# Three loads under way at a time, and two rows spread by GpSimd, in a fused RWKV-6 and mixture-of-depths kernel

## The chip, the cores and the metric

The kernel runs on one core of one Trainium2 chip. The metric is the device time of one execution in microseconds (us), taken as the median of several executions; lower is better. The engines have short names in the profile: PE is TensorE (PEld its weight loads), DVE VectorE, ACT ScalarE, POOL GpSimd and SP SyncE, which here only issues DMAs.

## What is computed

The reference has two parts, one behind the other. The first is a recurrence over 768 tokens for 4 batches and 8 heads of width 48:

```python
for t in range(S):
    cur = np.einsum('bhd,bhe->bhde', u[None] * kt, vt)
    y[:, :, t] = np.einsum('bhd,bhde->bhe', rt, state + cur)
    state = wt[:, :, :, None] * state + np.einsum('bhd,bhe->bhde', kt, vt)
```

Its result, laid out as 4 x 768 rows of 384, goes into the second part, in which the 128 tokens with the highest scores of each batch pass through a small network:

```python
scores = np.einsum('bsd,d->bs', x, w_gate)
top_idx = np.argpartition(-scores[b], capacity)[:capacity]
h = np.maximum(x[b, top_idx] @ w1, 0.0)
g = 1.0 / (1.0 + np.exp(-scores[b, top_idx]))
out[b, top_idx] = x[b, top_idx] + g[:, None] * (h @ w2)
```

Two small inputs matter for the change: `u`, 384 numbers that multiply r times k for every token, and `w_gate`, 384 numbers for the score. Both are needed as the same row in all 128 partitions.

## The kernel before

Time is cut into 24 chunks of 128 tokens (4 batches of 6), and the recurrence is done chunk by chunk with matmuls. One long loop at the end of the function, `for n in range(-4, N)`, is a software pipeline: iteration n works on chunk n's result and, ahead of it, on the stages of chunks n+1 to n+4. The order of the instructions on every engine is the order of the calls, written out by hand under `manual_schedule`.

The stages of one chunk, in order, with the lines by which the profile knows them:

- `load` (L110) issues one DMA of 192 KB from SP for each of w, k, r and v. `loads(n)` asks for v of chunk n+1, k and r of n+3 and w of n+4; iteration n calls `loads(n + 3)` near its end (a little differently in the first few). There are 96 such loads. Five w buffers and six each for k with r, and for v, rotate; a load waits until its buffer's last reader is done.
- `lnw` (L148) takes the logarithm of w on ACT. `sums` (L171) adds it up over the tokens on PE, and ACT takes the exponential (L173). `totals` (L183, L187) makes one line of 384 numbers on ACT and spreads it by a small DMA, issued from ACT, into `all_buf`. `without` (L194, DVE) and `falls` (L200, ACT) make the second exponential.
- `scaled` (L232, DVE) multiplies k and r by the exponentials. `own_products` (L209, L210) computes r times k times `u_bc` on POOL; `own_sum` (L217) adds it up per head on DVE; `own_values` (L224) multiplies by v on POOL.
- `turned` (L243, L245) transposes on PE and copies on ACT. `scores` (L259), `fresh` (L275), `masked` (L287, DVE), `states` (L300, L305 on DVE, L307 on POOL), `from_state` (L318) and `from_chunk` (L335) are the chunk's matmuls and what lies between them.
- `result` (L349, L355) adds the parts on DVE, forms the scores with `wg_bc`, and issues the chunk's store from ACT (L359).

From n = 6 on, steps of the second part (choosing rows, gathering them by a POOL DMA, two matmul layers at L485 and L495) are mixed in between by `mix`; those of the last batch make a tail with no chunk work beside it. From n = 7 on, eight DMAs of 384 KB from SP (L610) bring the weights of the network.

All DMA issues of SP and of ACT share eight semaphores, given out in turn when the program is compiled. An issue on either engine therefore also waits until the earlier transfer with the same semaphore, as a rule the eighth in front in the order of the program, has landed.

Before the loop ACT issues the loads of the rows `u_row` and `wg_row` into partition 0. POOL fills constants with memset and iota (L539 to L561). The rows are spread to all partitions inside the loop's first two iterations by `to_all` (L155, L156): PE multiplies a column of ones by the row into PSUM, and ACT copies the result to `u_bc` and `wg_bc`.

Of the kernel before, what the change touches and what calls it, by code (L numbers as in the profile page):

```python
# [9 lines left out]
FP32 = mybir.dt.float32  # L10
# [7 lines left out]
L = 128  # L18
# [4 lines left out]
def _rows(ap, n):  # L23

    return dataclasses.replace(ap, ap=[[0, n]] + [list(x) for x in ap.ap])
# [10 lines left out]
def kernel(  # L36
# [14 lines left out]
    nc = tc.nc  # L51
# [3 lines left out]
    C = H * D  # L55
# [13 lines left out]
    consts = ctx.enter_context(tc.tile_pool(name="consts", bufs=1))  # L69
# [6 lines left out]
    psM = ctx.enter_context(tc.tile_pool(name="psM", bufs=1, space=PSUM))  # L76
# [9 lines left out]
    u_bc = consts.tile([L, H, D], FP32)  # L86
    wg_bc = consts.tile([L, C], FP32)
    u_row = consts.tile([1, H, D], FP32)
    wg_row = consts.tile([1, C], FP32)
    ones_row = consts.tile([1, L], FP32)  # L90
    kr_bufs = [consts.tile([L, 2, H, HB], FP32, name=f"kr_buf{i}") for i in range(4)]
    line_bufs = [consts.tile([1, 2, HB, HP], FP32, name=f"line_buf{i}") for i in range(3)]
    p_bufs = [psP.tile([L, 2, 512], FP32, name=f"ps_p{i}") for i in range(2)]
    all_bufs = [consts.tile([L, HP], FP32, name=f"all_buf{i}") for i in range(6)]

    work = {n: {} for n in range(N)}
    latest = {}

    def load(name, n):
        if not 0 <= n < N:  # L100
            return
        b, ci = chunks[n]
        x, bufs = dict(w=(w, 5), k=(k, 6), r=(r, 6), v=(v, 6))[name]
        if name == "k":
            work[n]["kr"] = lev.tile([L, 2, H, D], FP32, tag="kr", name="kr", bufs=bufs)
        if name in "kr":
            t = work[n]["kr"][:, "kr".index(name)]
        else:
            t = lev.tile([L, H, D], FP32, tag=name, name=name, bufs=bufs)
        nc.sync.dma_start(  # L110
            out=t, in_=x[b, :, ci * L:(ci + 1) * L, :].rearrange("h t d -> t h d")
        )
        work[n][name] = t

    def loads(n):
        load("v", n + 1)
        load("k", n + 3)
        load("r", n + 3)
        load("w", n + 4)
# [18 lines left out]
    row = setup.tile([L, L], INT32)  # L138
# [5 lines left out]
    def lnw(n):  # L144
        if 0 <= n < N:
# [2 lines left out]
            nc.scalar.activation(  # L148
                out=t["lw"], in_=t.pop("w").rearrange("p h d -> p (h d)"), func=AF.Ln
            )  # L150

    def to_all(out, row):

        ps = psM.tile([L, 512], FP32, tag="f", name="ps_b")
        nc.tensor.matmul(ps[:, 0:C], ones_row, row, start=True, stop=True)  # L155
        nc.scalar.copy(out=out, in_=ps[:, 0:C])  # L156

    def sync(ins, on, why):

        tc.add_manual_dep(  # L160
            ins.ins, on.ins.name,
            mybir.DependencyInfo(mybir.DependencyClass.Sync, mybir.DependencyReason.DATA),
            reason=why,
        )

    def sums(n):
        if not 0 <= n < N:
# [81 lines left out]
    def half(i, n=HB):  # L249
        return slice(HB * i, HB * i + n)  # L250
# [201 lines left out]
    def gates(b):  # L452

        xe, gate = chosen[b][2], chosen[b][4]
        own = mod.tile([L, 1], FP32, name="own", bufs=2)
        scr = lev.tile([L, C], FP32, tag="scr", name="scr")
        nc.vector.tensor_tensor_reduce(
            out=scr, in0=xe, in1=wg_bc, scale=1.0, scalar=0.0, op0=ALU.mult, op1=ALU.add,
            accum_out=own,
        )  # L460
        neg = mod.tile([L, 1], FP32, name="neg", bufs=2)
        nc.vector.scalar_tensor_tensor(
            out=neg, in0=own, scalar=-1.0, in1=own, op0=ALU.mult, op1=ALU.min
        )
        yield
        nc.scalar.activation(out=neg, in_=neg, func=AF.Exp)
        yield
        den = mod.tile([L, 1], FP32, name="den", bufs=2)
        nc.vector.tensor_scalar_add(out=den, in0=neg, scalar1=1.0)
        nc.vector.reciprocal(out=den, in_=den)  # L470
        nc.vector.scalar_tensor_tensor(
            out=gate, in0=own, scalar=0.0, in1=neg, op0=ALU.is_ge, op1=ALU.max
        )
        nc.vector.tensor_mul(gate, gate, den)
        yield
# [55 lines left out]
    with tc.manual_schedule():  # L531
        nc.scalar.dma_start(out=u_row, in_=_rows(u, 1))
        nc.scalar.dma_start(out=wg_row, in_=_rows(moe_w_gate, 1))
        nc.scalar.preload_act_table_set("natural_log_exp_and_others")
        loads(-4)
        loads(-3)
        loads(-2)

        nc.gpsimd.memset(ones_row, 1.0)  # L539
        nc.gpsimd.iota(row, pattern=[[1, L]], base=0, channel_multiplier=0)  # L540
        nc.gpsimd.iota(col, pattern=[[0, L]], base=0, channel_multiplier=1)
        nc.vector.tensor_tensor(out=tri, in0=col, in1=row, op=ALU.is_ge)
        nc.vector.tensor_tensor(out=ident, in0=col, in1=row, op=ALU.is_equal)
        for t in kr_bufs:
            nc.vector.memset(t[:, :, :, D:HB], 0.0)
        for t in line_bufs:
            nc.gpsimd.memset(t[:, :, D:HB, :], 1.0)
        nc.vector.tensor_tensor(out=behind[:, 0:L], in0=col, in1=row, op=ALU.is_lt)
        for i in (0, 1):
            nc.vector.tensor_copy(out=mask[half(i)], in_=behind[half(i), half(i)])  # L550
            nc.vector.memset(p_bufs[i], 0.0)
        nc.vector.tensor_copy(out=slots, in_=row)
        nc.vector.memset(ones, 1.0)
        nc.vector.memset(ones_f, 1.0)
        nc.gpsimd.memset(behind[:, L:S], 1.0)
        nc.gpsimd.iota(count, pattern=[[-L, NCH]], base=S - 1, channel_multiplier=-1)
        nc.vector.tensor_copy(out=behind_n, in_=count)
        nc.gpsimd.iota(
            number[:, :, :, 0], pattern=[[S, B], [L, NCH]], base=0, channel_multiplier=0
        )  # L560
        nc.gpsimd.iota(  # L561
            number[:, :, :, 1], pattern=[[0, B], [0, NCH]], base=0, channel_multiplier=1
        )
        nc.vector.tensor_copy(out=ids, in_=number)

        for n in range(-4, N):
            what = ("", "", "")
            if n >= NCH:
                b, j = n // NCH - 1, n % NCH
                what = plan[j]  # L570
                if j == 0:
                    steps["s"] = select(b)
                if j == rank_at:
                    steps["x"] = chosen_rows(b, "m" if b == B - 2 else "f")
                if j == gate_at and b > 0:
                    steps["g"] = gates(b - 1)
            if n == N - 1:
                what = ("g", "", "g")
            from_state(n)
            own_values(n + 1)  # L580
            totals(n + 3)
            without(n + 3)
            lnw(n + 4)
            if n == -4:
                to_all(u_bc.rearrange("p h d -> p (h d)"), u_row.rearrange("o h d -> o (h d)"))
            scores(n + 1)
            fresh(n + 1)
            from_chunk(n)
            turned(n + 2, "K")
            turned(n + 2, "R")  # L590
            falls(n + 3)
            if n == -3:
                to_all(wg_bc, wg_row)
            masked(n + 1)
            states(n + 1)
            result(n)
            mix(what[0])
            if n >= 2 * NCH and n % NCH == 0:
                steps["f"] = forward(n // NCH - 2)
            sums(n + 4)  # L600
            mix(what[1])
            scaled(n + 3)
            mix(what[2])
            own_products(n + 3)
            own_sum(n + 2)
            for m in range(max(n - 1, -4) if n <= AHEAD else n, n if n < AHEAD else n + 1):
                loads(m + AHEAD)
            if 0 <= n - WEIGHTS_AT < len(weights):
                to, of = weights[n - WEIGHTS_AT]
                nc.sync.dma_start(out=to, in_=of)  # L610

        steps["s"] = select(B - 1)
        steps["x"] = run(steps["x"], chosen_rows(B - 1, "r"))
        mix("ffsxffsssssf")
        steps["f"] = forward(B - 2, "rmf")
        total = setup.tile([L, 1], FP32)
        nc.vector.tensor_reduce(out=total, in_=guard, axis=AX.XY, op=ALU.add)
        mix("ffffxxxff")
        ps = bank("f")
        nc.tensor.matmul(ps[0:1, 0:1], total, ones_f, start=True, stop=True)  # L620
        wide = setup.tile([1, 1], INT32)
        mix("xx")
        nc.vector.tensor_scalar(
            out=wide, in0=ps[0:1, 0:1], scalar1=LIMIT, scalar2=0.5, op0=ALU.is_le, op1=ALU.is_lt
        )
        steps["g"] = gates(B - 2)
        mix("gggff")
        wide = nc.values_load(wide, min_val=0, max_val=1)
        mix("fffffxffff")
        steps["g"] = gates(B - 1)  # L630
        mix("ggg")
        for _ in forward(B - 1, "mrf"):
            pass
# [104 lines left out]
```

## Time and profile before

| | |
|---|---|
| median of 3 runs | 187.31 us (186.99 to 192.36) |
| time of the profiled execution | 188.42 us |
| its span, first to last instruction | 186.5 us |
| PE busy | 162.9 us (87%) |
| DVE busy | 137.4 us (74%) |
| POOL busy | 92.9 us (50%) |
| ACT busy | 84.7 us (45%) |
| loads and weights (queue q1): share of the 16 DMA engines over the span | 57.5% |
| stores and small lines (queue q10): the same | 8.1% |
| landing of a load after its issue, median by tensor | 4.3 to 5.0 us, the shortest 3.0 us |

"Busy" is the time in which an engine had an instruction running. The digit rows of the profile cut the span into 40 slices of 4.66 us and give the busy share of each slice in tenths. The chain of waits goes back from the last instruction to whatever released it, and so on to the start; "issue" in it is time for which the profile shows no cause. A line of the timeline has the start and the duration in us, the engine and line, the operation, what it writes and reads, and in brackets the idle time before it and what ended it. "SPq" and "ACTq" are the sequencers that issue DMAs; the duration there is that of issuing, not of the transfer.

### The profile page before, as it was taken

The numbers are of one execution on the slowest core, as the hardware profiler recorded it, in microseconds if no ns is written. First come the engines' busy times: TensorE is split into PE (matmuls) and PEld (weight loads), VectorE is DVE, ScalarE is ACT, GpSimd is POOL, SyncE is SP. The second block draws the span as 40 slices with busy tenths as digits, with TensorE's granted clock in tenths as the row PEclk, the third lists the DMA queues.
The fourth block names the chain that finished last, engine by engine and source line by source line (L and its number), as shares of the span: only waits on it lengthen the run. The fifth ranks groups of instructions, "written<-read, shape, count | busy, mean of one in ns | idle before, by whom it ended". The sixth has DMA issues, their size and how long they took to land.

```text
span 186.5 us, 8415 instructions
## 1 busy us (share of the span) xinstructions
PE 162.9 (87%) x3590; PEld 131.2 (70%) x3590; DVE 137.4 (74%) x326; ACT 84.7 (45%) x239; POOL 92.9 (50%) x114
## 2 busy tenths in 40 slices
PE   4989959878995989895887999999999999999990
PEld 1358838657784777674777988768899867977940
DVE  6636978786879899998698789779999964942100
ACT  4476643565673736453753547257633303111200
POOL 4036776463765466589076255854756540131102
PEclk9999987999999999999999999999999999999997
DMA  6999987998999998999999999996111112020101
GB/s 125 210 197 187 179 171 169 212 212 182 206 189 202 225 231 223 183 241 226 215 208 260 226 197 270 219 190 150 43 49 46 47 48 84 0 91 4 42 9 46
DMA packets 109425, 28.98 MB, mean 155 GB/s; under 512 B 103362, under 2 KB 108996, under 8 KB 109380
## 3 DMA queue, kind: packets, MB, share of 16 engines
q1 hardware_dynamic: 102528, 22.03, 57.5%
q10 hardware_dynamic: 6340, 4.77, 8.1%
q0 software_dynamic: 512, 1.57, 2.5%
q8 instruction: 30, 0.49, 1.1%
q14 instruction: 15, 0.12, 0.2%
HBM read 22.81 MB, written 5.51 MB: 152 GB/s over the span
## 4 chain that ended last, share of the span: by engine, by line
PE 57%; issue 17%; POOL 5%; DMA 5%; DVE 4%; ACT 4%; ACTq 1%; POOLq 1%; DVEq 0%
PE ps_p L335 10%; PE ps_t L243 9%; PE ps_f L485 8%; PE ps_x L171 6%; PE ps_f L495 6%; PE ps_p L318 6%; PE ps_p L259 5%; PE ps_p L275 4%; DMA kr<-in_r_dram 3%; DMA all_buf<-line_buf 2%; POOL rk L209 2%; DVE kr_buf L232 1%; POOL vo L224 1%; PE ps_e L373 1%; PE ps_r L406 1%
## 5 line engine op out<-in xcount | busy, mean ns | idle before, releaser
L209 POOL TENSOR_TENSOR rk<-kr 128x384 f32<-128x384 f32 x24 | 24.0, 1001 | 51.6 <-DVE kr_buf L232 23.6
L335 PE MATMUL ps_p<-v,sc 64*64 64x48 f32 x768 | 28.7, 219 | 7.9 <-issue 4.2
L232 DVE TENSOR_TENSOR kr_buf<-kr,e 128x768 f32<-128x768 f32 x24 | 25.0, 1043 | 13.6 <-ACT e L200 11.9
L335 PEld LDWEIGHTS ps_p<-v,sc 64*64 64x64 f32 x768 | 25.4, 135 | 9.3 <-issue 4.9
L243 PE MATMUL ps_t<-ident,kr_buf 128*128 128x128 f32 x192 | 28.3, 292 | 2.0 <-issue 2.0
L245 ACT COPY Kt<-ps_t 128x512 f32<-128x512 f32 x24 | 14.0, 582 | 26.9 <-PE ps_t L243 26.9
L171 PE MATMUL ps_x<-lw,tri 128*128 128x384 f32 x48 | 23.3, 570 | 3.1 <-ACT lw L148 2.2
L243 PEld LDWEIGHTS ps_t<-ident,kr_buf 128*128 128x128 f32 x192 | 22.0, 147 | 4.5 <-issue 2.4
L210 POOL TENSOR_TENSOR rk<-rk,u_bc 128x384 f32<-128x384 f32 x24 | 24.0, 1002 | 1.9
L485 PEld LDWEIGHTS ps_f<-xeT,w 128*128 128x128 f32 x192 | 22.6, 192 | 1.3
L485 PE MATMUL ps_f<-xeT,w 128*128 128x128 f32 x192 | 23.4, 277 | 0.0
L495 PE MATMUL ps_f<-w,hid 128*128 128x384 f32 x64 | 22.2, 490 | 0.0
L224 POOL TENSOR_TENSOR vo<-v,own 128x384 f32<-128x384 f32 x24 | 20.2, 843 | 1.8 <-DVE own L217 1.8
L318 PEld LDWEIGHTS ps_p<-s,Rt 48*64 48x64 f32 x704 | 14.0, 138 | 10.0 <-issue 4.5
L148 ACT ACTIVATE lw<-w 128x384 f32<-128x384 f32 x24 | 12.6, 526 | 16.1 <-issue 5.5
L318 PE MATMUL ps_p<-s,Rt 48*64 48x48 f32 x704 | 17.3, 226 | 0.9 <-issue 0.5
L355 DVE CUSTOM_DVE_ANT_0 scr<-x,wg_bc 128x384 f32<-128x384 f32 x24 | 17.3, 722 | 0.8
L506 POOL DMA_INDIRECT out_dram<-ye,idx x4 | 4.7, 1173 | 26.3 <-DVE ye L503 15.6
L259 PE MATMUL ps_p<-Rt,Kt 48*64 48x64 f32 x768 | 17.7, 229 | 0.0
L173 ACT ACTIVATE e<-ps_x 128x384 f32<-128x384 f32 x24 | 11.7, 489 | 12.8 <-DVE score L355 3.5
L387 DVE SCALAR_TENSOR_TENSOR ahead<-every,score,behind 128x768 bf16<-128x768 f32 (+5 forms) x24 | 15.3, 679 | 2.6 <-ACT every L376 2.6
L287 DVE TENSOR_TENSOR sc<-ps_p,mask 128x512 f32<-128x512 f32 x24 | 16.3, 680 | 0.5 <-PE ps_p L275 0.5
(79 smaller groups left out, 247.5 us busy)
## 6 DMA issues: line engine op xcount, KB each, us to landing
w<-in_w_dram SPq DMA_DIRECT2D x24, 192.0 KB, 4.5
kr<-in_k_dram SPq DMA_DIRECT2D x24, 192.0 KB, 4.9
kr<-in_r_dram SPq DMA_DIRECT2D x24, 192.0 KB, 5.0
v<-in_v_dram SPq DMA_DIRECT2D x24, 192.0 KB, 4.3
out_dram<-x ACTq DMA_DIRECT2D x24, 192.0 KB, 3.8
w<-in_moe_w_dram SPq DMA_DIRECT2D x8, 384.0 KB, 5.8
all_buf<-line_buf ACTq DMA_DIRECT2D x20, 2.0 KB, 3.5
xe<-out_dram,idx POOLq DMA_INDIRECT x4, 4.2
```

The costliest lines, as they stand in the source:

```text
L171: nc.tensor.matmul(ps[:, 0:C], tri, t["lw"], start=True, stop=True)
L209: sync(nc.gpsimd.tensor_mul(rk, t.pop("r"), t.pop("k")), latest["two"], "one port")
L210: nc.gpsimd.tensor_mul(rk, rk, u_bc)
L224: nc.gpsimd.tensor_mul(t["vo"], t["v"], t.pop("own").to_broadcast([L, H, D]))
L232: latest["two"] = nc.vector.tensor_mul(both[:, :, :, 0:D], t.pop("kr"), t.pop("e").rearrange("p q (h d) -> p q h d", d=D),)
L243: nc.tensor.transpose(ps[:, j, :], t[name][:, 2 * j:2 * j + 2, :], ident)
L259: nc.tensor.matmul(P[half(sub), par, j * HB:(j + 1) * HB], t["Kt"][half(par, D), j, half(sub)], t["Rt"][half(par, D), j, half(sub)], start ...
L318: nc.tensor.matmul(t["P"][half(sub), par, j * D:(j + 1) * D], t["Rt"][half(par, D), j, half(sub)], t["s1" if sub else "s0"][half(par, D), ...
L335: nc.tensor.matmul(t["P"][half(sub), par, j * D:(j + 1) * D], t["sc"][half(sub), par, j, :], t["v"][half(sub), 2 * j + par, :], start=(sub ...
L355: nc.vector.tensor_tensor_reduce(out=scr, in0=x, in1=wg_bc, scale=1.0, scalar=0.0, op0=ALU.mult, op1=ALU.add, accum_out=score[:, b, ci:ci ...
L485: nc.tensor.matmul(ps[:, q, :], w1[:, dc, (f0 + q) * L:(f0 + q + 1) * L], xeT[:, dc, :], start=(dc == 0), stop=(dc == NDC - 1),)
L495: nc.tensor.matmul(ps, hid[:, fc, :], w2[:, fc, :], start=(fc == 0), stop=(fc == NFC - 1))
```

## The change

`load` keeps a list of the loads' issue instructions. From the 17th load on, each load gets a dependency on the third load in front of it: it is issued after that one has landed. The weights' DMAs (L610) and ACT's DMAs are not in the list. `to_all` with its matmuls and ACT copies goes, and so does the row of ones. In its place POOL runs two `partition_broadcast` instructions ahead of the loop, after its last iota. `sync`, the helper that adds a dependency, moves up unchanged.

```diff
+    under_way = []
+    MOST = 3
+    UNLIMITED = 16
...
-        nc.sync.dma_start(
+        under_way.append(nc.sync.dma_start(
             out=t, in_=x[b, :, ci * L:(ci + 1) * L, :].rearrange("h t d -> t h d")
-        )
+        ))
+        if len(under_way) > UNLIMITED:
+            sync(under_way[-1], under_way[-1 - MOST], "loads under way")
...
-    def to_all(out, row):
-
-        ps = psM.tile([L, 512], FP32, tag="f", name="ps_b")
-        nc.tensor.matmul(ps[:, 0:C], ones_row, row, start=True, stop=True)
-        nc.scalar.copy(out=out, in_=ps[:, 0:C])
...
-        nc.gpsimd.memset(ones_row, 1.0)
...
         nc.vector.tensor_copy(out=ids, in_=number)
+        nc.gpsimd.partition_broadcast(
+            u_bc.rearrange("p h d -> p (h d)"), u_row.rearrange("o h d -> o (h d)"), channels=L
+        )
+        nc.gpsimd.partition_broadcast(wg_bc, wg_row, channels=L)
...
-            if n == -4:
-                to_all(u_bc.rearrange("p h d -> p (h d)"), u_row.rearrange("o h d -> o (h d)"))
...
-            if n == -3:
-                to_all(wg_bc, wg_row)
```

More of the change, by code (lines that the diff above doesn't have):

```diff
@@ L89 @@
     wg_row = consts.tile([1, C], FP32)
-    ones_row = consts.tile([1, L], FP32)
     kr_bufs = [consts.tile([L, 2, H, HB], FP32, name=f"kr_buf{i}") for i in range(4)]
@@ L96, with sync @@
     work = {n: {} for n in range(N)}
+    under_way = []
+    MOST = 3
+    UNLIMITED = 16
     latest = {}
+    def sync(ins, on, why):
+        tc.add_manual_dep(
+            ins.ins, on.ins.name,
+            mybir.DependencyInfo(mybir.DependencyClass.Sync, mybir.DependencyReason.DATA),
+            reason=why,
+        )
     def load(name, n):
@@ L150, in lnw @@
             )
-    def to_all(out, row):
-        ps = psM.tile([L, 512], FP32, tag="f", name="ps_b")
-        nc.tensor.matmul(ps[:, 0:C], ones_row, row, start=True, stop=True)
-        nc.scalar.copy(out=out, in_=ps[:, 0:C])
[L158 to L164, printed above, removed]
     def sums(n):
@@ L564 @@
         nc.vector.tensor_copy(out=ids, in_=number)
+        nc.gpsimd.partition_broadcast(
+            u_bc.rearrange("p h d -> p (h d)"), u_row.rearrange("o h d -> o (h d)"), channels=L
+        )
+        nc.gpsimd.partition_broadcast(wg_bc, wg_row, channels=L)
         for n in range(-4, N):
```

## The prediction

> **What bounds the kernel now.** I read the digit rows first, for the stages:
>
> ```profile
> PE   4989959878995989895887999999999999999990
> DVE  6636978786879899998698789779999964942100
> POOL 4036776463765466589076255854756540131102
> DMA  6999987998999998999999999996111112020101
> ```
>
> Up to slice 27 (some 126 us) the 16 DMA engines are nearly full and so is PE; behind it PE works alone through the second part. Queue q1 holds 57.5% of 186.5 us = 107.2 us for 96 loads and 8 weight transfers, so one transfer keeps the engines 1.03 us. A chunk of four loads and a store (8.1% of 186.5 over 24 = 0.63 us) needs 4.75 us. From chunk 3 to chunk 10 `kr_buf` (L232) starts at 22.06 and 61.83 us: 5.68 us a chunk. In the same window PE's own work for a chunk, summed from the chain's pieces (L243 1.02, L171 0.65, L318 0.61, L259 0.48, L275 0.36, L335 0.93), is 4.05 us. DMA has some 0.9 us a chunk to spare there, little more than PE.
>
> Next the chain of waits, cut to 22 to 32 us:
>
> ```profile
> 23.78 0.48 PE ps_t L243 x3
> 24.26 2.04 issue
> 26.30 0.71 PE ps_t L243 x5
> ```
>
> PE stands for 2.04 us in the middle of a row of transposes. Of such "issue" gaps the groups of L335, L243, L275 and L318 have 4.2 + 2.0 + 2.3 + 0.5 = 9.0 us, and the timeline shows none over 0.3 us after 125 us, when the loads are over.
>
> Then SP's timeline, for what limits loads today:
>
> ```profile
> 22.20 0.92 SPq L110 DMA_DIRECT2D w<-in_w_dram  x1
> 23.16 2.96 SPq L110 DMA_DIRECT2D v<-in_v_dram  x1
> 26.21 0.56 SPq L110 DMA_DIRECT2D kr<-in_k_dram  x1
> ```
>
> An issue that takes 0.4 us when nothing is queued takes 2.96: the queue is full and pushes back. And ACT's timeline:
>
> ```profile
> 92.11 0.47 ACT L183 ACTIVATE line_buf<-ps_x 1x384 f32<-1x384 f32 x1
> 93.97 0.48 ACTq L187 DMA_DIRECT2D all_buf<-line_buf  x1
> 94.49 0.52 ACT L148 ACTIVATE lw<-w 128x384 f32<-128x384 f32 x1 [1.91 <-DMA kr<-in_r_dram]
> ```
>
> ACT stood 1.91 us until an r load landed, which none of its data needs: its own DMA issue uses that load's semaphore. Late loads reach ACT through this too.
>
> Last, the prologue, POOL and DVE:
>
> ```profile
> 2.61 0.14 POOL L561 IOTA number<- 128x24 int32 x1
> 8.93 1.00 POOL L209 TENSOR_TENSOR rk<-kr 128x384 f32<-128x384 f32 x1 [6.18 <-DVE kr_buf L232]
> ...
> 13.71 0.55 DVE L217 TENSOR_REDUCE own<-rk 128x8 f32<-128x384 f32 x1
> 14.18 0.55 DVE L194 TENSOR_TENSOR less<-ps_x,lw 128x384 f32<-128x384 f32 x1
> ```
>
> POOL idles 6.18 us, from 2.75 to 8.93, so a new instruction there seems free. Chunk 0's product ends at 11.0 and DVE adds it up only at 13.71: 2.7 us more of slack. But DVE runs in order, and `less` of chunk 2, which ACT and PE need, stands right behind.
>
> **What the Trainium skill says.** "GPSIMD Engine Reference", section 2.1 (Instruction dispatch): GpSimd's instructions are software that can be loaded at run time, and the first call to a freshly loaded kernel pays about 6 us (5.95 measured) with no instruction of its own in the profile. No such load is in this trace (the iota at L540 starts 0.06 us after the memset before it), so nothing here agrees or disagrees. "DMA: Bandwidth & Descriptors", section Anatomy of one DMA: about 2.0 us of a DMA are fixed, most of it the receipt that the last byte is written. The trace agrees: the first w load is issued at 0.76, ACT uses it at 3.78, so 3.02 us, less 1.03 of transfer. "Runtime: NRT & Kernel Launch", section Instruction fetch mechanics: instructions come by DMA in blocks of 16 KiB, as a rule hidden. Queue q8 moved 30 packets, 0.49 MB, 16 KB each; PE's gaps beside full DMA engines suggest that hiding fails there.
>
> **The change part by part.** *Removed from PE and ACT.* Two pairs of matmuls (L155, 1.61 and 1.64 us a pair) and two copies of 0.46 us. The first pair runs 2.26 to 3.87, before the first `ps_x` at 4.35, which waits for w: nothing. The second ends at 7.57 where `ps_x` could have gone at 7.23 (its input is ready then): 0.3 us gained at most. ACT's copies lie in idle time; ones_row's memset was 0.19 us on an idle POOL. Take -0.3.
>
> *Added to POOL.* Two broadcasts of 384 columns. Nearest rows: an iota of 128 columns 0.22 us, so 0.66 for 384; a two-input product of 384 columns 1.00. Take 0.6 each, 1.2 together, between 0.5 and 2 us. Both rows' DMAs landed by 3.3 us (2.0 at most after issue), so they hardly wait. Alone they would end at about 4, well ahead of 8.93: nothing.
>
> *Added unseen.* The kernel used only memset, iota, tensor_tensor and indirect DMA on POOL. If partition_broadcast lives in another loaded set than tensor_tensor, POOL must load one before it and the old one after it. Price: 6 us each by the page; other transfers take longer beside full DMA engines (an all_buf line lands in 2.0 us at best, 3.5 in the median; a store 1.9 and 3.8), so I take 9, between 6 and 12. Then POOL's first product starts at 2.75 + 9 + 1.2 + 9 = 22 and DVE's L217 at 24.1, against 13.71: DVE and all behind it are 10.4 us late. With 6 us each it is 4.4, with 12 it is 16.4; with a single load 1.4. Behind POOL's stall wait `own`, `vo`, `s` (L307), and so PE and ACT. SP meanwhile runs on only until it meets buffers and semaphores that ACT has to pass, about eight transfers. What is won back: for seven chunks up to 62 us the period can fall from 5.68 to about 5.1 (4.05 of PE work and the issue gaps, near DMA's 4.75), 0.6 x 7 = 4 us. Later there is no room: DVE is at 95% in 60 to 75 us and PE at 96% from 95 to 125. Net +6, between +1 and +12.
>
> *The limit.* From load 17 (15.16 us) to the 55th (62.75) SP issued one load per 1.25 us. With three under way the rate is three per landing time: at the unloaded 3.02 us one per 1.02, no limit; at the median of all loads, 4.8 (the view of L110), one per 1.6, so 6.4 us a chunk against 5.68 and +13 us in 38 loads. Fewer in front make landings shorter, so I take the middle, 3.9, one per 1.3: +2 us, half of it hidden by data loaded ahead during POOL's stall: +1. What waits behind a held load on SP: the next loads, and from 64 us on the weights, uncounted, which keep the engines filled; a chunk then lasts some 6.4 us and needs 5.2 of loads. Who waits for SP: ACT's L148 and its issues L187 and L359. Where less is queued, instruction fetches may come sooner: a tenth of the 9.0 us, -0.5.
>
> *Sum.* -0.3 + 0 + 6 + 1 - 0.5 = +6.2. On the profiled execution, span 186.5 and time 188.42, that is 194.6; that execution is 1.1 above the median of 187.31, so I forecast 193.5.
>
> **Rivals.** *A, faster.* The broadcast needs no load, and a shorter queue cures the gaps in PE: 60% of 9.0 us and 0.3, so 181.6. For it: the gaps lie only where loads run. Against: the limit still leaves a load or two queued. It decides where landings fall to 3.1 us or so: then three under way feed a load per 1.03 us, the engines stay full, and fetches wait less. *B, slower by the limit.* No load of programs, but landings stay near 4.8 us because stores and weights share the engines: +5 to +13, 192 to 200. For it: the windows give the DMA engines a share of 0.94 or more in every stretch from 4 to 125 us but one (0.85 in 30 to 40); any gap between loads is lost for good. *C, nothing happens.* The full queue and the eight semaphores already hold loads to about four under way (issued 1.25 us apart, landing after 4.8: 3.8 on the mean), so three changes nearly nothing, and the broadcast is cheap: 187. *D, dear loads:* 12 us each: 199 to 200.
>
> **How the numbers follow.** Two program loads, with or without a little from the limit: 0.50. D: 0.08; B: 0.10; A: 0.18; C or a single load: 0.14. Two per cent, 3.7 us, is about what a measurement of this kernel can tell from no change: faster below 183.6, slower above 191.1. The forecast's own case reaches below 191.1 only with short loads, which I count under C. So faster 0.18, within 0.14, slower 0.68. The likeliest case alone spans 190 to 198. The range must take in C and the mildest of A at its lower end and all but the top of B and D at its upper: 184 to 199. Outside remain most of A (0.13) and some of B and D (0.06).
>
> **What would show it.** Right: on POOL an idle stretch of 15 us or more around the two broadcasts, the first product at 16 us or later, L217 late by as much, a `less` waiting behind it; then a period of about 5 us. Wrong: broadcasts done by 5 us and the first product at 8.9. For the limit: median landings of 3.5 to 4 us, issues no longer 2 to 3 us long, DMA digits down to 8 in 15 to 60 us; wrong if the digits stay 9 and landings stay 4.8. For A: PE's issue gaps below 4 us in sum.

## The result: slower, 199.96 us against 187.22

The changed kernel takes 199.96 us (median of 4 runs, 199.75 to 200.14); the kernel before, 187.22 us. The ratio is 1.068, 95% interval 1.066 to 1.071: 12.7 us more. The forecast was 193.5 with a range up to 199, so the direction was right, and the time lies just outside the range. Some executions of one kernel last a few per cent longer than its others: medians here and below hold all, ratios and their intervals leave those out, and a dash in the table below stands for a profile of one of them.

In the profiled execution (200.14 us, span 198.4) the lines have moved: `load` is L120, `lnw` L160, the first exponential L171, the `all_buf` line L181 and L185, `own_products` L207 and L208, `own_sum` L215, `scaled` L230, `from_chunk` L333, the store L357. First the digit rows, 40 slices of 4.96 us:

```profile
PE   1670898797697768796699996999999999999990
DVE  6530889697566999987579995757999993861201
POOL 3204957484651766549415775175477622040202
...
DMA  6999998789998799898997997962120112111101
```

Two things differ. In the fourth slice (15 to 20 us) PE and DVE stand still while the DMA engines go on. And from the eighth slice to the end of the loads DMA has 7s, 8s and 6s where it had 9s, and PE has 6s and 7s up to 100 us. The timeline of POOL and DVE around the first of these:

```profile
2.68 0.14 POOL L558 IOTA number<- 128x24 int32 x1
8.51 1.07 POOL L563 PARTITION_BROADCAST u_bc<-u_row  x1 [5.68 <-issue]
9.46 0.67 POOL L566 PARTITION_BROADCAST wg_bc<-wg_row  x1
17.37 0.98 POOL L207 TENSOR_TENSOR rk<-kr 128x384 f32<-128x384 f32 x1 [7.24 <-issue]
...
19.45 0.55 DVE L215 TENSOR_REDUCE own<-rk 128x8 f32<-128x384 f32 x1 [5.56 <-POOL rk L208]
```

POOL idles 5.68 us before the first broadcast and 7.24 us behind the second, with nothing in the timeline to wait for. The list of the instructions of L563 and of L207 has a pair of MODIFY_POOL_CONFIG, of POOL's sequencer, at the head of each of the two stretches (2.8 and 10.0 us). I read the stretches as two loads of programs. DVE's L215 starts at 19.45 where it started at 13.71, 5.7 us late, and behind it in DVE's order stands `less`, for which ACT and PE wait. For the second, the chain of waits (start, duration, what) in a stretch of the weights' loads:

```profile
74.67 6.02 DMA kr<-in_k_dram
...
80.84 4.82 DMA v<-in_v_dram
...
87.35 7.22 DMA kr<-in_k_dram
...
94.65 0.41 ACTq L357
95.06 0.05 issue
95.11 0.58 ACT e L171 x2
...
95.79 1.39 PE ps_p L333 x32
```

Loads follow one another on the path, each issued when an earlier one lands. Then comes a store's issue on ACT (L357), 0.08 us after the k load of 87.35 has landed. ACT needs nothing of that load: `kr_buf` reads it at 112.85, 18 us later. The store uses its semaphore: by the trace's semaphore numbers the DMAs of SP and ACT share eight, those of GpSimd have eight others, and at least 12 of ACT's 44 issues inside the loop start within 0.15 us of the landing of an SP load on the same semaphore. Behind the store in ACT's order stand the exponential (L171) and `seen`, a small copy out of `ps_p` between `from_state` and `from_chunk`, for which PE waits. The list of waits shows how often that happens (total us, times, longest):

```profile
PE ps_p L333 <- ACT seen L324: 9.7, 7, 2.4
ACT e L171 <- DMA kr<-in_k_dram: 6.4, 3, 3.3
ACT lw L160 <- DMA kr<-in_k_dram: 3.8, 2, 3.0
ACT lw L160 <- DMA w<-in_moe_w_dram: 2.0, 1, 2.0
ACT lw L160 <- DMA kr<-in_r_dram: 1.9, 3, 0.8
ACT lw L160 <- DMA v<-in_v_dram: 1.6, 1, 1.6
```

None of these ACT instructions reads k, r, v or a weight. With two more rows of `e` (v 0.9, r 0.8 us) ACT stood 17.4 us for transfers it doesn't use; in the kernel before it was 5.6 (v 2.1, r 1.9, w 1.0 ahead of an instruction that doesn't read it, k 0.6). PE's wait for `seen` grew to these 9.7 us from 3.7 in the kernel before:

```profile
PE ps_p L335 <- ACT seen L326: 3.7, 6, 1.9
```

### The profile page after: what moved, and what is told of

It is laid out like the page before. It is cut to its first block, busy times and chain, and to the rows that moved or that the text cites. A ratio compares the mean times of both kernels' runs of the same rounds, so it can differ in the third digit from the quotient of the medians.

```text
span 198.4 us, 8426 instructions
## 1 busy us (share of the span) xinstructions
PE 164.0 (83%) x3586; PEld 133.5 (67%) x3586; DVE 137.4 (69%) x326; ACT 84.6 (43%) x237; POOL 94.5 (48%) x115
## 4 chain that ended last, share of the span: by engine, by line
PE 35%; DMA 14%; issue 9%; DVE 4%; ACT 3%; POOL 1%; SPq 1%; POOLq 1%; ACTq 1%
DMA kr<-in_k_dram 7%; PE ps_p L333 6%; PE ps_f L483 6%; PE ps_f L493 5%; PE ps_t L241 5%; DMA kr<-in_r_dram 3%; PE ps_p L316 3%; PE ps_x L169 3%; DMA v<-in_v_dram 2%; PE ps_p L257 2%; DVE ahead L385 2%; DMA w<-in_w_dram 1%; PE ps_p L273 1%; DVE kr_buf L230 1%; DMA all_buf<-line_buf 1%
## 5 line engine op out<-in xcount | busy, mean ns | idle before, releaser
L207 POOL TENSOR_TENSOR rk<-kr 128x384 f32<-128x384 f32 x24 | 24.0, 998 | 48.4 <-DVE ahead L385 22.7
L333 PE MATMUL ps_p<-v,sc 64*64 64x48 f32 x768 | 29.3, 222 | 12.9 <-ACT seen L324 9.7
L169 PE MATMUL ps_x<-lw,tri 128*128 128x384 f32 x48 | 25.0, 608 | 14.9 <-ACT lw L160 8.5
L333 PEld LDWEIGHTS ps_p<-v,sc 64*64 64x64 f32 x768 | 26.1, 137 | 14.4 <-ACT seen L324 10.7
L230 DVE TENSOR_TENSOR kr_buf<-kr,e 128x768 f32<-128x768 f32 x24 | 25.3, 1056 | 12.8 <-ACT e L198 10.6
L241 PE MATMUL ps_t<-ident,kr_buf 128*128 128x128 f32 x192 | 30.6, 310 | 0.5 <-DVE kr_buf L230 0.5
L241 PEld LDWEIGHTS ps_t<-ident,kr_buf 128*128 128x128 f32 x192 | 24.1, 158 | 2.9 <-DVE kr_buf L230 1.0
L208 POOL TENSOR_TENSOR rk<-rk,u_bc 128x384 f32<-128x384 f32 x24 | 24.0, 1000 | 1.9
L171 ACT ACTIVATE e<-ps_x 128x384 f32<-128x384 f32 x24 | 11.8, 491 | 23.2 <-DMA kr<-in_k_dram 6.4
L192 DVE TENSOR_TENSOR less<-ps_x,lw 128x384 f32<-128x384 f32 x24 | 13.2, 550 | 11.4 <-ACT line_buf L181 11.2
L169 PEld LDWEIGHTS ps_x<-lw,tri 128*128 128x128 f32 x48 | 8.8, 229 | 17.9 <-ACT lw L160 10.6
L160 ACT ACTIVATE lw<-w 128x384 f32<-128x384 f32 x24 | 12.6, 524 | 18.4 <-issue 4.3
L305 POOL TENSOR_TENSOR s<-mid,all_buf 128x192 f32<-128x192 f32 x20 | 15.0, 751 | 5.5 <-PE ps_p L333 3.4
L353 DVE CUSTOM_DVE_ANT_0 scr<-x,wg_bc 128x384 f32<-128x384 f32 x24 | 16.7, 695 | 0.8
```

The source lines that it names most:

```text
L169: nc.tensor.matmul(ps[:, 0:C], tri, t["lw"], start=True, stop=True)
L207: sync(nc.gpsimd.tensor_mul(rk, t.pop("r"), t.pop("k")), latest["two"], "one port")
L208: nc.gpsimd.tensor_mul(rk, rk, u_bc)
L230: latest["two"] = nc.vector.tensor_mul(both[:, :, :, 0:D], t.pop("kr"), t.pop("e").rearrange("p q (h d) -> p q h d", d=D),)
L241: nc.tensor.transpose(ps[:, j, :], t[name][:, 2 * j:2 * j + 2, :], ident)
L333: nc.tensor.matmul(t["P"][half(sub), par, j * D:(j + 1) * D], t["sc"][half(sub), par, j, :], t["v"][half(sub), 2 * j + par, :], start=(sub ...
```

## The experiments

Eighteen kernels, each beside runs of the kernel before on the same chip (one chip for e1 to e4, others for e5 to e8, e9 to e15 and e16 to e18); ratios are to those runs. "Late" is the start of `kr_buf` in the timeline of the profiled execution, less that of the kernel before (22.06, 78.39 and 142.04 us for chunks 3, 13 and 23).

| run | median us (range) | ratio, 95% interval | late at chunk 3, 13, 23 |
|---|---|---|---|
| the change | 199.96 (199.75 to 200.14) | 1.068, 1.066 to 1.071 | 6.0, 7.8, 11.8 |
| e1 limit alone | 196.56 (195.05 to 201.23) | 1.039, 1.026 to 1.052 | -0.2, 3.2, 6.6 |
| e2 broadcast alone | 196.61 (196.21 to 196.88) | 1.038, 1.029 to 1.048 | 6.1, 4.4, 8.4 |
| e3 limit, stores by GpSimd | 192.82 (191.69 to 195.17) | 1.017, 1.007 to 1.027 | – |
| e4 before, stores by GpSimd | 185.82 (184.63 to 189.01) | 0.978, 0.966 to 0.989 | -1.1, -2.9, -2.8 |
| e5 limit, no DMA on ACT | 189.08 (185.94 to 192.41) | 0.990, 0.986 to 0.995 | – |
| e6 before, no DMA on ACT | 185.63 (185.38 to 188.73) | 0.979, 0.970 to 0.989 | -1.6, -4.0, -4.8 |
| e7 limit of four | 190.96 (186.15 to 192.26) | none | – |
| e8 broadcast, programs kept | 192.90 (190.95 to 193.86) | 1.014, 1.002 to 1.026 | 5.4, 6.4, 4.1 |
| e9 broadcast, no DMA on ACT | 195.54 (193.81 to 196.94) | 1.031, 1.020 to 1.043 | 6.1, 5.9, 4.3 |
| e10 the change, no DMA on ACT | 193.99 (193.23 to 196.10) | 1.029, 1.020 to 1.039 | 7.3, 4.6, 2.7 |
| e11 rows by DMA, no DMA of chunks on ACT | 189.45 (187.67 to 193.58) | 1.002, 0.999 to 1.005 | 1.5, 2.8, -0.2 |
| e12 e6 without u product | 188.47 (185.39 to 192.14) | 0.990, 0.986 to 0.994 | – |
| e13 e12 and broadcast | 191.73 (189.70 to 192.35) | 1.013, 1.001 to 1.026 | 5.3, 4.8, 0.9 |
| e14 e12 and limit | 189.14 (187.08 to 192.96) | 0.999, 0.995 to 1.003 | – |
| e15 e12 and both | 190.77 (187.84 to 192.98) | 1.014, 1.002 to 1.026 | 5.4, 0.4, -2.6 |
| e16 before, lines by GpSimd | 188.18 (186.28 to 189.76) | 0.989, 0.982 to 0.995 | – |
| e17 early issues by GpSimd | 186.32 (184.68 to 187.94) | 0.980, 0.972 to 0.987 | -1.2, -2.2, -4.2 |
| e18 e6 again | 186.69 (184.28 to 187.44) | 0.979, 0.971 to 0.986 | – |

### Each part alone, and the stores moved

e1 is the kernel before with the list and the wait of `load` only, e2 the changed kernel without them:

```diff
-        if len(under_way) > UNLIMITED:
-            sync(under_way[-1], under_way[-1 - MOST], "loads under way")
```

e3 and e4 move ACT's store, in e1 and in the kernel before:

```diff
-        nc.scalar.dma_start(out=views[b][b, ci * L:(ci + 1) * L, :], in_=x)
+        nc.gpsimd.dma_start(out=views[b][b, ci * L:(ci + 1) * L, :], in_=x)
```

> The limit of three loads alone, with the rows still spread by PE and ACT. Theory T1 (the loss has two parts: POOL's stall of some 5.7 us, partly won back, and some 8 us of the limit): 194 to 196 us. Theory T2 (the recorded sum: the limit is worth +0.5, the whole loss is POOL's stall that is never won back): 187 to 189 us. Under T1 ACT's store issues wait for landings of k, r and v loads in most chunks, although these loads land 10 us or more before their use.

> The broadcast by GpSimd alone, loads without the limit. T1: 190 to 192 us, the first product on POOL at about 17.4 us as in the changed kernel. T2: 197 to 199 us.

> The limit alone, as e1, but the 24 stores of the result are issued from GpSimd, so that no store issue stands in ACT's order. Theory L1 (the limit costs because ACT's issues wait on held loads through shared semaphores): most of the loss of e1 goes, within 3 us of e4. Theory L2 (the limit starves the DMA engines, whose rate sets the pace): the same 6 to 9 us slower than e4 as e1 is than the kernel before.

> The kernel before with the 24 stores issued from GpSimd: the base for e3. Between 184 and 190 us: ACT loses its waits at the stores (some gain if they matter today), POOL gets about 1 us of issuing per chunk.

Measured: the limit costs 7.8 us and the broadcast 7.9, as medians beside 188.75, and 3.9 and 3.8% by the ratios. T1 had the limit nearly right and put the broadcast too low; T2 erred in the limit and came close for the broadcast. The sum, 15.7 us or 7.7%, is more than the 12.7 us or 6.8% of both together, but the intervals are wider than that difference: that the two share a cause is a hint here and no more. e3 lies 7.0 us over e4: with the stores moved the limit costs as much as ever, and L1, that the stores carry its cost, falls as it stood. But the lines (`all_buf`) were still issued by ACT, and in e3's profile (a dash in the table) `lw`, behind them in ACT's order, stands 10.8 us for k, r and v loads. The chain of waits of e1 shows the limit at work:

```profile
47.05 5.17 DMA v<-in_v_dram
...
52.30 0.40 ACTq L365
...
52.75 0.58 ACT e L179 x2
53.34 0.06 ACT seen L332
...
53.44 1.46 PE ps_p L341 x32
```

Again PE waits for ACT, ACT for a store's semaphore, and that for a v load that took 5.17 us to land.

### ACT issues no DMA

e5 (limit) and e6 (none) have the stores and the lines issued by GpSimd, whose DMAs don't take turns with SP's:

```diff
-        nc.scalar.dma_start(out=t["all"], in_=line.rearrange("o q d j -> o (q d j)"))
+        nc.gpsimd.dma_start(out=t["all"], in_=line.rearrange("o q d j -> o (q d j)"))
```

> The limit of three loads, rows by PE and ACT, and both kinds of DMA that ACT issued (24 stores, 20 all_buf lines) issued by GpSimd instead, so that ACT waits for no DMA semaphore of its own issues. Coupling theory: the limit costs time because ACT's issues take their turn of the eight semaphores behind loads that nobody needs yet; with none on ACT the limit costs under 2 us, so this run lies within 2 us of e6, at 184 to 189. Starvation theory: three loads under way leave the 16 DMA engines idle in part (share 0.79 to 0.86 with the limit alone), and the data come late; then this run is again 6 to 8 us over e6, and k and r loads land less than 3 us before their use in the chunks where time is lost.

> The kernel before with stores and lines both issued by GpSimd, no limit, rows by PE and ACT. Both theories need it as the other end of e5. With stores alone moved 185.8 was measured. If ACT's waits were what was won there, moving the lines as well wins 1 to 3 us more: 183 to 185.5. If GpSimd becomes the bound by the issues (it was busy 9.3 of 10 us in 20 to 30 us with the stores moved), it loses: 187 to 190.

The limit's cost fell from 3.9% to 1.1% (e5 beside e6 by their ratios, 2.0 us; the medians differ by 3.5), give or take some 1%. The waits of e6 and then of e5:

```profile
PE ps_p L335 <- ACT seen L326: 0.3, 1, 0.3
ACT lw L148 <- DMA w<-in_w_dram: 4.2, 6, 1.6
```

```profile
PE ps_p L341 <- ACT seen L332: 0.3, 1, 0.3
ACT lw L162 <- DMA w<-in_w_dram: 21.5, 12, 2.5
```

PE waits 0.3 us for `seen`, no longer 3.7 or 8.5 (e1). In e5 a different wait has come: `lw` stands 21.5 us for w, which it does read (e5 has a dash in the table; in e15, which has none, it is 12.1). So the coupling theory holds for most of the limit's cost: it went with ACT's issues. What is left may be data that come late.

### Four loads, and programs kept

e7 is e1 with `MOST = 4`. e8 is e2 with one line ahead of the broadcasts, which loads a set of GpSimd programs meant to hold the broadcast, iota and tensor_tensor:

```diff
+        nc.gpsimd.load_library(library_config.all_libraries[10])
         nc.gpsimd.partition_broadcast(
```

> The limit alone with four loads under way instead of three, ACT's issues as before. Both theories of the limit agree that it is dear because it is under what the kernel used: the loads before overlapped to 3.8 on the mean (4.8 us of landing, one issue per 1.25 us). With four the cost falls to 0 to 3 us: 187 to 191, DMA share of 0.88 or more in 30 to 60 us. If it stays at 195 or more, the number under way is not what costs, but the waits themselves on SP.

> The broadcast alone, no limit, but GpSimd is given, after the last iota and ahead of the broadcasts, one set of programs that holds the broadcast, the iota and tensor_tensor all, so it need not change back. If the two program loads are the whole cost of the broadcast (196.6 in e2): one idle stretch of 5 to 7 us on POOL, broadcasts done by 11, first product by 12, own's reduction (L213) by 14.5 at the latest, and a time of 187 to 190. If the cost comes from something else in the broadcast (its own 1.7 us, the rows' later arrival for DVE, or work lost late, at chunks 14 to 18): 193 to 197 with the second idle stretch gone.

e7's four runs lie between 186.15 and 192.26 us, too far apart for a verdict; in the profiled one SP needed 47.1 us from the 17th load to the 55th, as in the kernel before (47.6), where e1 needed 52.2. That the number under way sets the loads' pace is thus shown; the time at four is not. e8 didn't do what it was made for, as the timeline of its POOL shows:

```profile
8.00 0.23 POOL L535 IOTA row<- 128x128 int32 x1 [7.55 <-issue]
...
15.48 0.68 POOL L563 PARTITION_BROADCAST u_bc<-u_row  x1 [5.75 <-DMA kr<-in_r_dram]
16.05 0.67 POOL L566 PARTITION_BROADCAST wg_bc<-wg_row  x1
16.58 1.11 POOL L205 TENSOR_TENSOR rk<-kr 128x384 f32<-128x384 f32 x1
```

The idle stretch behind the broadcasts is gone, which shows that it was the change of sets; but one of 7.55 us stands ahead of the first iota, where e2 has none. A pair of MODIFY_POOL_CONFIG stands ahead of the first iota in the kernel before too, at 0.9 us, and there the iota starts at 1.0. As I read it, in e8 the execution before has left the other set loaded, and the first iota of the next one asks for the standard set again. So there are still two loads, of 7.55 and 5.75 us, and what one alone would cost was not measured. Of chunk 0's 6.6 us delay 4.1 are left at the end.

### The broadcast with ACT free, and rows by DMA

e9 and e10 are e2 and the changed kernel with e6's two edits. e11 is e6 with each row read 128 times by its own DMA:

```diff
-        nc.scalar.dma_start(out=u_row, in_=_rows(u, 1))
-        nc.scalar.dma_start(out=wg_row, in_=_rows(moe_w_gate, 1))
+        nc.scalar.dma_start(out=u_bc, in_=_rows(u, L))
+        nc.scalar.dma_start(out=wg_bc, in_=_rows(moe_w_gate, L))
```

> The broadcast by GpSimd alone (no limit), with ACT issuing no DMA (stores and lines issued by GpSimd). Beside e6 (185.6, the same without the broadcast). Coupling theory: of the broadcast's 7.9 us some 4 are lost at chunks 14 to 18 because ACT's issues wait for loads; without them only the stall of 5.7 us in the prologue is left, part of it won back as in the run with one load in front (6.6 us at chunk 0, 4.1 at the end): 189 to 191.5. If the broadcast costs its 7.9 whatever ACT issues: 193 to 194.5.

> The changed kernel, limit and broadcast both, with ACT issuing no DMA. Coupling theory: limit 2 to 3 us (e5 beside e6) and broadcast 4 to 5, against e6's 185.6: 190 to 194, so that the 12.7 us of the change shrink to 5 to 8. If ACT's waits are not what makes the change dear: 197 to 199.

> The candidate: no limit, stores and lines issued by GpSimd, and the rows of u and the gate spread by their own DMA, which reads one row 128 times, instead of PE and ACT or GpSimd. No program load on POOL, so the first product stays at 8 to 9 us. The theory that only the program loads make the broadcast dear expects e6's time or up to 1 us less: 184.5 to 186. If two more transfers of 192 KB in the prologue (1 us of the 16 engines each) push w and k back, chunk 0 is 2 us late: 186.5 to 188.

e10 lies at the upper end of what was expected, 6 us under the changed kernel; beside its own base, e6, the change costs 0.050 of the time, and not 0.068. e9 missed, at 195.5: its distance to e6 is 7.7 us at chunk 3 and 9.1 at chunk 23, so beside e6 nothing was won back. The answer for a window (20 to 45 us in e9: length, then busy time of PE, PEld, DVE, ACT and POOL) shows what else had changed:

```profile
20.00:45.00 25.00, 21.52 (x633) 17.60 (x633) 21.68 (x42) 13.22 (x42) 24.37 (x29) 0.90 0.98 203
```

POOL is busy 24.37 of 25 us (21.10 in e6, 15.70 in the kernel before): it had taken 44 issues of some 0.6 us, and might itself be the bound. e11 missed too: with the two transfers in front, `kr_buf` of chunk 0 is 2.9 us late.

### GpSimd relieved

e12 to e15 are e6, e9, e5 and e10 with GpSimd's second product left out; the multiplication by u is missing from their outputs.

```diff
         sync(nc.gpsimd.tensor_mul(rk, t.pop("r"), t.pop("k")), latest["two"], "one port")
-        nc.gpsimd.tensor_mul(rk, rk, u_bc)
```

> As e6 (no limit, rows by PE and ACT, stores and lines issued by GpSimd), but GpSimd's second product (rk by u, 1.0 us a chunk) is left out, so the output lacks u's part. It frees GpSimd, which worked without a pause from 17 to 45 us in e9. The base of three others. With GpSimd free the pace in 20 to 60 us can only be that of the DMA engines or PE: chunk period 4.8 to 5.1 us, 183 to 186.

> As e12, with the broadcast by GpSimd in place of PE and ACT. Theory W: the stall of the prologue (6 to 8 us at chunk 3) is won back in part once neither ACT waits for loads nor GpSimd is full, because loads ran on in the stall and lie ready: the difference to e12 shrinks from about 7 at chunk 3 to 4 or less at chunk 14. Theory N: it is kept in full, 6 us or more at chunk 14 and at the end, because PE, DVE or the DMA engines have no room in any case.

> As e12, with the limit of three loads. If what is left of the limit's cost without ACT's issues (2.8 us up to chunk 21 in e5 beside e6) is data that come late (ACT's lw stood 21.5 us for w in e5), it stays at 2 to 4 us here or grows, since GpSimd no longer hides it; lw waits for w in ten chunks or more. If it was GpSimd: 0 to 1 us.

> As e12, with both parts of the change. With ACT's issues both cost 12.7, in e10 without them 7.6 by chunk 23. If data are late by the limit only where the kernel has no lead, the stall's lead of loads hides it: e15 within 1.5 us of e13. If limit and stall each keep their own price: e15 = e12 plus the differences of e13 and e14.

In e13 POOL is busy 15.80 of the same 25 us. The base e12 missed: without the product it is no faster than e6 (0.990 of the kernel before, e6 0.979), so GpSimd alone was not what held e6. By the ratios the broadcast now costs 2.3% (e9 beside e6: 5.2%), the limit 0.9%, both together 2.4%; by the medians 3.3, 0.7 and 2.3 us. Each carries an uncertainty of some 1%, e15 rests on two executions, and e14 lies between its two expectations. The timelines agree: between chunks 3 and 23 e13 wins 4.4 us on the kernel before (5.3 late, then 0.9) and e15 8.0, e9 1.8 and e10 4.6, where e2 loses 2.3 and the change 5.8. Theory W holds: beside e12 (a dash in the table) e13 is 6.6 us late at chunk 3, 4.3 at chunk 14 and 2.7 at chunk 23. So the change, 6.8% as it was made, costs some 2% where ACT waits for no load and GpSimd isn't full. (With the product left out and the issues kept on ACT nothing was run; there GpSimd isn't full anyway, at 15.70 of 25 us in the kernel before.) The waits of e15:

```profile
ACT lw L160 <- DMA w<-in_w_dram: 12.1, 11, 3.0
...
PE ps_p L332 <- ACT seen L323: 0.3, 1, 0.3
```

### Which of ACT's issues, and a faster version

e16 moves the lines alone. e17 is e6 with the late issues left on ACT (`nc.gpsimd if n < 20 else nc.scalar` for the stores, 22 for the lines).

> The kernel before with the lines alone (20 all_buf transfers of 2 KB) issued by GpSimd, the stores still by ACT. Both kinds moved gained 3.2 us (e6), the stores alone 2.9 (e4). A line's issue stands ahead of lw on ACT, a store's at the end of ACT's chunk. If either kind of wait alone is enough to hold ACT to the pace of the loads, this gains little, 0 to 1.5 us: 187 to 189; if waits add up, some 1 to 2 us: 186 to 187.5.

> The candidate: the kernel before, with the stores of chunks 0 to 19 and the lines up to chunk 21 issued by GpSimd and the later ones by ACT, where the loads are over and ACT's issues wait for nothing. e6 lost 0.8 us of its lead at chunks 22 and 23, where GpSimd's issues stand between its products, and 2.1 us after the last scatter. The first is saved, of the second a part at most: 184 to 185.5, that is 0.2 to 1.5 us under e6. If the late issues cost nothing: as e6.

> e6 once more, in five rounds and on one chip with the two others, for its ratio to the kernel before: 0.975 to 0.985, and the 2.1 us that its end takes longer after the last scatter.

The lines alone gain 0.011 of the time, the stores alone 0.022 (e4, another chip), both 0.021: the stores seem the greater part, though the intervals overlap. e17 and e18 cannot be told apart, so the late issues are worth less than these runs can tell. With no DMA on ACT the kernel beats the one before by 2.1% (e6 and e18, intervals 1.1 to 3.0% and 1.4 to 2.9%), and the changed one by far.

## Why the forecast was wrong

**The program loads were there.** "If partition_broadcast lives in another loaded set than tensor_tensor, POOL must load one before it and the old one after it": so it was. Each was put at 9 us, and they took 5.7 and 7.2. The six microseconds of the Trainium skill ("GPSIMD Engine Reference", section 2.1, Instruction dispatch) were nearer than the surcharge I laid on it for full DMA engines. The broadcasts took 1.07 and 0.67 us, against 0.6 each. So the first product started at 17.4 and not at 22, and L217 was 5.7 us late and not 10.4.

**"What is won back" was the first step that failed.** Of the 10.4 us, 4 were to come back, by a period of 5.1 us made of "4.05 of PE work and the issue gaps". That work was read too low. In the same seven chunks of the kernel before (22.06 to 61.83 us) PE was busy 32.10 of 39.77 us, 4.6 us a chunk (3.4 us of it at half clock, see below), and 7.4 of the other 7.7 us were "issue" gaps. So PE had no room for a shorter period unless the gaps shrank. In e2 they did (3.9 us from chunk 3 to 13, against 7.9): the period fell to 5.40 us from chunk 3 to 10, and 1.7 us had come back by chunk 13. Then 4.0 us were lost again by chunk 23, where the prediction saw no room to win but no loss either. The forecast also saw ACT's wait ("its own DMA issue uses that load's semaphore") and named L187 and L359 as those who wait for SP, but gave it no price. Two errors in one term, a delay too long and a recovery that didn't last, nearly cancelled: +6 was forecast, and +7.9 measured. That was luck.

**"The limit" was the second, and the larger.** The pace was nearly right: one load per 1.3 us was forecast, and in e1 SP needed 52.2 us from the 17th load to the 55th, or 1.37 for each of 38, against 1.25 before. Median landings fell to 3.6 to 4.3 us in the changed kernel (3.9 was taken). Wrong was "half of it hidden by data loaded ahead during POOL's stall: +1". Data were ahead: after the first chunks, k, r and v landed 11 to 24 us before their use in the changed kernel. It hid nothing, because ACT's issues waited for landings and not for needs. Also, what stood "from 64 us on the weights, uncounted, which keep the engines filled" cost on: of e1's 6.6 us at chunk 23, 3.4 came behind chunk 13, where many loads took 5 to 7 us to land beside the weights. The term was +7.8 alone, not +1; on top of the broadcast 199.96 is 3.4 us more than e2's 196.61, and 3.0% more by the ratios, read across two chips.

**The clock of PE had no term.** The rows of the granted clock, of the kernel before and of the changed one:

```profile
PEclk9999987999999999999999999999999999999997
PEclk9998599999799999889799999699999999999997
```

The changed kernel's PE got half its clock for 6.8 us from 18.0 us on, and for 3.4 us each from 52.1, 82.8, 96.5 and 123.8; the kernel before only for 3.4 us from 26.9, the end of the span apart. Each stretch began in a pause of PE or up to 1.1 us behind one: in the changed kernel pauses of 5.5, 2.1, 1.3, 2.4 and 1.7 us, the last four for `seen`. Not every such pause had one behind it: that of 2.3 us up to 58.3 us in the kernel before had none. From chunk 3 to chunk 23 the changed kernel took 5.9 us longer, and PE's busy time, for the same work, was 4.3 us longer (109.5 us against 105.2); only 1.6 us were more idle time. In e1 it was 4.2 of 6.8 us, and in e2 all of 2.3. So in these profiles a wait of PE cost more than its own length, and a good part of what is put down to waits here was slower matmuls behind them. No run kept the clock up to test this, the ends of matmuls are modelled, and over whole runs the time doesn't follow the clock closely: beside e1 the kernel before took 188.99 us at 0.996 and 188.41 at 0.959.

**The fetch gaps.** -0.5 was taken. PE's "issue" gaps did fall, from 9.0 to 3.3 us in the changed kernel, below the 4 us that were to speak for rival A, and the time rose all the same: PE's waits for `seen` grew by 6.0 us. Nor is the limit a cure for them: e5, with the limit, has 10.9. That the gaps are instruction fetches no run here shows.

**The rivals.** B was true as to the limit's size (+5 to +13) and had the wrong way to it: the DMA engines did stand idle more, at a share of 0.81 in 30 to 40 us (0.85 before), but the path went through ACT. D gave 199 to 200, which is the time measured, for loads of 12 us which were not there: a chance hit. What the prediction left out is the case in which both costs come in full; it spoke of "with or without a little from the limit". The signs named in advance held for the digits, the landings and the first product; the idle stretch around the broadcasts was 12.9 us and not 15, the period was 5.79 us from chunk 3 to 10 and not about 5, and of 18 load issues that took over 1.5 us 9 were left, the longest 3.3 us. One sum is off without effect on the result: "one transfer keeps the engines 1.03 us" counts a weight transfer of 384 KB like a load of 192. By bytes a load takes 0.96 us, and a chunk needs 4.5 us and not 4.75.

**Still open.** What made e2 lose 4.2 us between chunks 13 and 18 is shown in part. PE was busy 29.1 us there, against 26.5 in the kernel before, at a mean granted clock of 0.90 against 1.00, behind a wait of 2.0 us for `seen` and an "issue" gap of 2.7. e9 and e13, whose ACT issues no chunk's DMA, lose nothing there, at a clock of 1.00; whether ACT's issues or chance made the difference in clock wasn't tried. That a stall isn't won back because of ACT's issues alone isn't shown either: e9 won nothing back beside e6, and e13 left out a product as well. That the limit's rest (e5, 2.0 us) is late w, is argued from `lw`'s wait and wasn't tried with more w buffers; e5's PE also had 6.8 us at half clock from 55.7 us on, e6's none before the end.

## What to carry to other kernels

Ask of every engine that issues a DMA which earlier transfer its issue must wait for: a store on a computing engine can tie it to the newest load, and then slack in the data hides nothing. A limit on loads under way should be priced at this wait first, and an engine that takes over issues should be looked at for room. Before counting on a stall to be won back, take an engine's work per chunk from its busy time in a window, and look at the granted clock behind each pause of PE. Before the first use of another GpSimd instruction, look for the sets of programs: what was a free slot for 1.7 us of work became a stall of 14.6 us.

## What the runs showed that I had not expected

- A set of GpSimd programs took 5.7 to 6.2 us to change to and 7.2 to 7.8 to change back (in the seven runs with the broadcast), and it seems to stay from one execution to the next (the 7.55 us ahead of e8's first iota).
- The more DMAs GpSimd issued, the longer was the end. From the start of the last scatter to the end of the span: 4.0 us in the kernel before and 4.1 in the changed one, 4.7 with 20 such issues (e16), 4.8 with 24 (e4), 5.7 with 38 (e17), 6.2 with 44 (e6, e10, e18).
